# Sigmoid attention and an MLP on one core: the keys in chunks of 128 rows, the last 64 rows of two heads together

## The chip, the cores and the metric

The kernel runs on one NeuronCore of a Trainium2 chip. The metric is device time in microseconds (us). Three timed runs of the kernel before gave 1116.61 to 1118.22 us, median 1117.94.

## The reference

```python
B, H, S, D = 8, 12, 448, 64
scores = q @ k.T / sqrt(D) - log(S)            # per batch and head
attn   = sigmoid(scores)
y      = attn @ v
x = y.transpose(0, 2, 1, 3).reshape(B * S, H * D)     # 3584 tokens of 768
h = x @ w_in                                   # 768 -> 2048
g = h * sigmoid(1.702 * h)
out = g @ w_out                                # 2048 -> 768
```

q, k, v and x are float32. The two weight matrices come as float64; they go to the chip as pairs of 32-bit words and are made into float32 there. There is no softmax, so a row of scores needs no maximum and no sum.

## The kernel before

**Number formats.** Most products run in a rounded float32 format (`F32R`). A float32 operand is split into a rounded part and a rest, and a product is three matmuls: high by rest, rest by high, high by high. The product of attention and v is done in plain float32, for which TensorE gets two instructions per product.

**The attention.** The work is cut into 48 pairs of heads (8 batches by 6 pairs). Of a pair, q and k lie with the depth on the partitions, head 0 in partitions 0 to 63 and head 1 in 64 to 127, q in columns 0 to 447 and k in columns 448 to 895 of one tile. `split_pair` splits that tile (a cast, on ScalarE or VectorE, L340 or L341, and a subtraction on VectorE, L346). k's 448 rows are cut into NC = 4 chunks of C = 112 rows. For each chunk, `scores` (L518) issues three times two matmuls: those of the two heads use 64 rows of the array each, one the upper and one the lower half, and write two PSUM banks. One sigmoid on ScalarE (L529) reads both banks, 112 partitions by 896 columns. `values` (L541) then multiplies v's chunk by this: head 0 writes partitions 0 to 63, head 1 partitions 64 to 127 of one bank, with 112 rows of the array and 64 columns each. After the four chunks, that bank is copied into the tokens' tiles (L575 on ScalarE, L577 on VectorE), in one or two pieces, because a batch has 448 tokens and a block of the MLP has 512.

**PSUM banks.** Of the eight banks, six hold scores: tag `sc` has two buffers of two banks, tag `sc3` one, and the chunks take them in turn (`next(chunks) % 3`), whatever the pair. The other two, `av` and `m0`, take the sums of `values` of the odd and the even pairs.

**The order on TensorE.** A unit of the attention is the four chunks of scores of pair n, then the four chunks of values of pair n-1. The first units of the MLP (`h`, L686) may be placed between, but only at the end, since they need tokens and banks.

**The weights.** 32 tiles of weights, 768 KB each as float64, are loaded and decoded during the attention by some eight small operations each on VectorE and ScalarE (L393 to L427). The float32 result is stored to DRAM, and for half of them sums of weights are formed and stored as well.

**The planner.** `Plan` runs a list of tasks against costs given in the code and records, engine by engine, the order in which they are emitted; the order is then fixed. DMAs are all issued by SyncE, in one order. ScalarE, VectorE and SyncE take, of the tasks that are ready, the one whose result is needed soonest on TensorE. A load of weights has as its place in that list the split of a pair `PACE * i + 2` (`firsts`, the splits in order); it may be issued earlier if one of three buffers is free.

**The rest.** After the attention the MLP runs in blocks of tokens: block 0 by plain products (`h` and `o`), the others two at a time by a Strassen-like scheme (`two_blocks`). All its matmuls use 128 rows and 128 columns of the array and 512 moving columns.

Of the kernel before, what the change touches and what calls it, by code (L numbers as in the profile page):

```python
# [9 lines left out]
F32 = mybir.dt.float32  # L10
# [6 lines left out]
U64 = mybir.dt.uint64  # L17
AF = mybir.ActivationFunctionType
ALU = mybir.AluOpType

P = 128


T = 512

PACE = 1.3


SOON, PATIENCE = 6, 0.8
# [6 lines left out]
    sc=2, sc3=1, av=1, m=2, m0=1,  # L36
# [29 lines left out]
class Plan:  # L66
# [10 lines left out]
    def buffer(self, tag):  # L77
        b = Buffer()
        self.rings.setdefault(tag, []).append(b)
        return b  # L80

    def task(self, engine, cost, emit, deps=(), uses=()):
        return self.either({engine: cost}, {engine: emit}, deps, uses)
# [159 lines left out]
def sigmoid_attention_mlp(ctx: ExitStack, tc: tile.TileContext, qk, v, w, out):  # L243
# [2 lines left out]
    D = 64  # L246
    H = HD // D
    NP = H // 2
    S = S2 // 2
    NB = out.shape[0]  # L250
    NM = out.shape[1]
    NK = H * D // P
    NW = w.shape[0]
    NF = NW * NK // (NK + NM)

    NC = 4
    C = S // NC
    NW_EL = NK * P
    scale = 1.0 / math.sqrt(D)
    neg_log_s = -math.log(S)  # L260
# [45 lines left out]
    def make(b, tag, shape, dtype, name):  # L306
        if tag == "m" and tag not in spaces:
            early_bank.close()
            banks(tag, early_bank)
        if tag in LATE and tag not in spaces:  # L310
            att_stack.close()
            late = late_stack.enter_context(tc.tile_pool(name="late", bufs=2))
            for t in LATE:
                spaces[t] = late
        b.tile = spaces.get(tag, sb).tile(shape, dtype, tag=tag, name=name, bufs=BUFS[tag])
        return b.tile

    def dma(into, src, kb, deps, uses, first=lambda: None):
        def emit():
            first()  # L320
            nc.sync.dma_start(out=into(), in_=src())  # L321

        return task("SP", kb, emit, deps, uses)
# [48 lines left out]
    def decode(n):  # L372

        tag = "raw64"
        raw, e, sg = buffer(tag), buffer("e"), buffer("e")

        def take():
            make(raw, tag, [P, 2 * NW_EL], F32, f"w64_{n}")

        def words():  # L380
            r = raw.tile.bitcast(U64)
            pair = r.bitcast(U32).rearrange("p (n t) -> p n t", t=2)
            top = r.bitcast(U16).rearrange("p (n t) -> p n t", t=4)[:, :, 3]
            return pair[:, :, 0], pair[:, :, 1], top

        load = dma(lambda: raw.tile.bitcast(U64), lambda: w[n], 2 * KB, [], [raw], take)
        load.landing += 1.5
        plan.early.append((load, firsts[min(2 + int(PACE * len(decoded)), len(firsts) - 1)]))


        def exponent():
            make(e, "e", [P, NW_EL], U16, f"expo{n}")
            nc.vector.tensor_scalar(e.tile, words()[2], 0x7FF0, None, op0=ALU.bitwise_and)  # L393

        def sign():
            make(sg, "e", [P, NW_EL], BF16, f"sign{n}")
            nc.scalar.activation(sg.tile, words()[2].bitcast(I16), AF.Sign)  # L397

        t_e = task("DVE", 0.56, exponent, [load], [e, raw])
        t_s = task("ACT", 0.92, sign, [load], [sg, raw])  # L400
        t_b = task("DVE", 0.35, lambda: nc.vector.tensor_scalar(
            e.tile, e.tile, 896.0 * 16, 1151.0 * 16, op0=ALU.max, op1=ALU.min), [t_e], [e])
        t_x = on_either(
            (0.84, lambda: nc.scalar.activation(e.tile, e.tile, AF.Copy, scale=8.0, bias=-896.0 * 128)),
            (0.35, lambda: nc.vector.tensor_scalar(
                e.tile, e.tile, 896.0 * 16, 8.0, op0=ALU.subtract, op1=ALU.mult)),
            [t_b], [e],
        )
        t_g = task("DVE", 0.56, lambda: nc.vector.tensor_tensor(
            e.tile.bitcast(BF16), e.tile.bitcast(BF16), sg.tile, op=ALU.mult), [t_x, t_s], [e, sg])  # L410


        f = buffer("g")

        def f32():
            return f.tile[:, :NW_EL]

        def mantissa():
            make(f, "g", [P, 2 * T], F32, f"w32_{n}")
            nc.vector.tensor_scalar(  # L420
                f32().bitcast(U32), words()[1], 0xFFFFF, 0x100000, op0=ALU.bitwise_and, op1=ALU.bitwise_or
            )

        t_m = task("DVE", 0.56, mantissa, [load], [f, raw])
        t_l = task("DVE", 0.96, lambda: nc.vector.scalar_tensor_tensor(
            f32(), words()[0], 2.0**-32, f32().bitcast(I32), op0=ALU.mult, op1=ALU.add), [t_m], [f, raw])
        t_p = task("DVE", 0.96, lambda: nc.vector.scalar_tensor_tensor(  # L427
            f32(), f32(), 2.0**-20, e.tile.bitcast(BF16), op0=ALU.mult, op1=ALU.mult), [t_l, t_g], [f, e])
        decoded[n] = (t_p, f, f32)
        stored[n] = dma(lambda: whole[n], f32, KB, [t_p], [f])  # L430

    def two_parts(b, name, n, f, f32, deps):

# [40 lines left out]
    def load_pair(b, p):  # L474

        tag = "x"
        qkr, vr = buffer(tag), buffer("vraw")
        vals, rows = v[b], C
        t_q = dma(lambda: qkr.tile, lambda: qk[b, p * P : (p + 1) * P], P * S2 * 4 / 1024, [], [qkr],
                  lambda: make(qkr, tag, [P, S2], F32, f"qkraw{b}_{p}"))  # L480
        t_v = dma(lambda: vr.tile[:rows], lambda: vals[:, 2 * p : 2 * p + 2], rows * 8 * D * 4 / 1024, [], [vr],
                  lambda: make(vr, "vraw", [P, 2, NC, D], F32, f"vraw{b}_{p}"))
        return t_q, qkr, t_v, vr

    def split_pair(b, p, t_q, qkr):
# [7 lines left out]
        )  # L493
        return t, s


    chunks = itertools.count()
    last_early = []

    def scores(b, p, c, t_s, s, a):  # L500

        tag = "sc"
        if next(chunks) % 3 == 2:
            tag = "sc3"
        ps = buffer(tag)
        if tag == "sc3":
            last_early[:] = [ps]


        plain = (b, p) == (0, 0)  # L510
        terms = ((0, 0),) if plain else ((0, 1), (1, 0), (0, 0))

        def emit():
            make(ps, tag, [P, 2, 512], F32, f"sc{b}_{p}_{c}")
            src = [s.tile] if plain else [s.tile[:, 0], s.tile[:, 1]]
            for n, (kk, qq) in enumerate(terms):
                for j, rows in enumerate(halves_of_rows):
                    nc.tensor.matmul(  # L518
                        ps.tile[:C, j, :S],
                        lhsT=src[kk][rows, S + c * C : S + (c + 1) * C], rhs=src[qq][rows, :S],  # L520
                        start=n == 0, stop=n == len(terms) - 1,
                    )

        t = task("PE", 0.9 if plain else (0.7, 0.61, 0.61, 0.7)[c], emit, [t_s], [ps, s])

        def sigmoid():
            if a.tile is None:
                make(a, "a", [P, 2, 2, S], F32, f"a{b}_{p}_{c}")
            nc.scalar.activation(  # L529
                a.tile[:C, c % 2], ps.tile[:C, :, :S], AF.Sigmoid, bias=bias[:C], scale=scale  # L530
            )

        return t, task("ACT", 1.02, sigmoid, [t], [a, ps])

    def values(b, p, c, t_a, a, t_v, vr, ps, bank):

        def emit():
            if c == 0:
                make(ps, bank, [P, 512], F32, f"av{b}_{p}")
            for j, cols in enumerate(halves_of_rows):  # L540
                nc.tensor.matmul(  # L541
                    ps.tile[cols, :S], lhsT=vr.tile[:C, j, c], rhs=a.tile[:C, c % 2, j],
                    start=c == 0, stop=c == NC - 1,
                )

        return task("PE", (0.8, 0.75, 0.75, 0.85)[c], emit, [t_a, t_v], [ps, a, vr])

# [54 lines left out]
    def attention():  # L602

        units, late = [], []
        for n, (b, p) in enumerate(pairs):
            t_q, qkr, t_v, vr = load_pair(b, p)
            t_s, s = split_pair(b, p, t_q, qkr)
            bank = "av" if n % 2 else "m0"
            ps = buffer(bank)
            scored, next_late = [], []  # L610
            firsts.append(t_s)
            for half in range(2):
                a = buffer("a")
                got = [scores(b, p, c, t_s, s, a) for c in range(2 * half, 2 * half + 2)]
                scored.append([g[0] for g in got])
                next_late.append([
                    values(b, p, 2 * half + i, g[1], a, t_v, vr, ps, bank) for i, g in enumerate(got)
                ])

            for t in scored[1]:  # L620
                t.alone = False
            units.append(scored[0] + scored[1] + [t for two in late for t in two])
            to_x(b, p, next_late[1][1], ps)
            late = next_late
        units.append(late[0] + late[1])
        return units
# [545 lines left out]
```

## Time and profile before

| what | value |
|---|---|
| the profiled execution's own time | 1117.21 us |
| its span, first to last instruction | 1115.4 us |
| median of three timed runs | 1117.94 us |
| granted TensorE clock | 1.00 |
| TensorE matmuls busy | 1107.6 us (99%) |
| VectorE busy | 759.4 us (68%) |
| ScalarE busy | 508.1 us (46%) |
| first scores to the first `h` of the MLP | 4.25 to 295.47 us |

How to read it: the busy time of TensorE's matmuls (PE in the profile) says little here, since a matmul's end is modelled and one overlaps the next; how far apart two matmuls start says more. PEld is the loading of weights into the array. A group's row has the number of instructions, the busy time of the group and the mean of one, and behind the second bar the idle time of that engine just before them with what ended it. In a row of the timeline the first number is the start, the second how long the row lasts, both in us; equal instructions that follow each other make one row.

### The profile page before, as it was taken

To read this page: it belongs to the slowest core of one execution; us is meant where nothing else is said; L and a number is where in the kernel's file an instruction comes from. 1 tells how busy PE (TensorE), PEld (TensorE's weight loads), DVE (VectorE), ACT (ScalarE), POOL (GpSimd) and SP (SyncE) were. 2 spreads that over 40 slices of the span, in tenths; PEclk is the share of its full clock that TensorE was granted. 3 is DMA by queue.
4 is the path that set the end of the run, shared out by engine and by line. 5 is a ranking of instruction groups with operands and counts; after the bars stand their busy time and mean duration, and the time that the engine had idled before them with its cause. 6 is when DMAs were issued, how large, how long until landed. Compare 5 with 4: busy or idle time off the path is not lost.

```text
span 1115.4 us, 14973 instructions
## 1 busy us (share of the span) xinstructions
PE 1107.6 (99%) x5517; PEld 819.6 (73%) x5517; DVE 759.4 (68%) x1234; ACT 508.1 (46%) x729; POOL 0.2 (0%) x4
## 2 busy tenths in 40 slices
PE   8999999999999999999999999999999999999998
PEld 3544544545688888888888888888888888888887
DVE  6999999895496426887984664448864744477652
ACT  6988988888563322223633222225432322244220
POOL 0000000000000000000000000000000000000000
PEclk9999999999999999999999999999999999999999
DMA  9999999995455968666777975567669755556665
GB/s 330 333 375 375 388 400 395 385 338 162 151 188 182 358 216 321 246 244 216 254 227 223 307 242 191 195 198 250 216 208 310 255 188 191 195 174 214 207 202 194
DMA packets 113097, 285.69 MB, mean 256 GB/s; under 512 B 10368, under 2 KB 51328, under 8 KB 113024
## 3 DMA queue, kind: packets, MB, share of 16 engines
q1 hardware_dynamic: 113024, 284.73, 74.6%
q8 instruction: 44, 0.72, 0.3%
q14 instruction: 29, 0.24, 0.1%
HBM read 206.05 MB, written 78.64 MB: 255 GB/s over the span
## 4 chain that ended last, share of the span: by engine, by line
PE 96%; ACT 1%; DMA 1%; issue 0%; DVE 0%; SPq 0%; ACTq 0%; DVEq 0%
PE os L1059 18%; PE m L918 18%; PE oa L1059 13%; PE av L541 13%; PE sc L518 11%; PE sc L918 9%; PE h L686 6%; PE o L686 6%; PE av L918 4%; DMA qkraw<-qk 1%; ACT a L529 1%; SPq L321 0%; ACT sign L397 0%; DVE qk L346 0%; ACT qk L340 0%
## 5 line engine op out<-in xcount | busy, mean ns | idle before, releaser
L529 ACT ACTIVATE a<-sc,bias 112x896 f32<-112x896 f32 x192 | 183.0, 1006 | 42.8 <-PE av L541 30.4
L1059 PE MATMUL os<-gs,wds 128*128 128x512 f32 x864 | 196.3, 389 | 0.0
L1059 PEld LDWEIGHTS os<-gs,wds 128*128 128x128 f32 x864 | 162.2, 188 | 33.7
L541 PE MATMUL av<-a,vraw 112*64 112x448 f32 x768 | 154.7, 545 | 0.0
L1059 PE MATMUL oa<-ga,wda 128*128 128x512 f32 x648 | 147.4, 389 | 0.0
L1059 PEld LDWEIGHTS oa<-ga,wda 128*128 128x128 f32 x648 | 121.6, 188 | 25.3
L518 PE MATMUL sc<-qk 64*112 64x448 f32 x1128 | 137.4, 378 | 2.2 <-ACT a L529 2.1
L518 PEld LDWEIGHTS sc<-qk 64*112 64x112 f32 x1128 | 90.9, 171 | 63.3 <-ACT a L529 52.0
L541 PEld LDWEIGHTS av<-a,vraw 112*64 112x64 f32 x768 | 50.9, 136 | 82.3 <-issue 73.4
L918 PE MATMUL m<-x_s,w 128*128 128x512 f32 x468 | 109.3, 389 | 0.0
L918 PE MATMUL sc<-x,w 128*128 128x512 f32 x432 | 105.7, 389 | 0.0
L918 PEld LDWEIGHTS m<-x_s,w 128*128 128x128 f32 x468 | 87.8, 188 | 18.2
L918 PEld LDWEIGHTS sc<-x,w 128*128 128x128 f32 x432 | 81.1, 188 | 16.8
L880 ACT ACTIVATE g<-h 128x512 f32<-128x512 f32 x72 | 44.7, 632 | 91.1 <-DVE h L781 90.3
L340 ACT CAST gs<-gs 128x512 fp32r<-128x512 f32 x75 | 46.6, 623 | 84.5 <-PE os L1059 74.5
L686 PE MATMUL h<-x,wsplit 128*128 128x512 f32 x288 | 65.6, 389 | 0.0
L686 PE MATMUL o<-gs,wsplit 128*128 128x512 f32 x288 | 65.4, 389 | 0.0
L686 PEld LDWEIGHTS h<-x,wsplit 128*128 128x128 f32 x288 | 54.0, 188 | 11.9 <-issue 0.7
L686 PEld LDWEIGHTS o<-gs,wsplit 128*128 128x128 f32 x288 | 54.1, 188 | 11.2
L346 DVE TENSOR_TENSOR gs<-gs,gs 128x512 fp32r<-128x512 f32 x96 | 60.9, 686 | 0.4
L885 DVE TENSOR_TENSOR gs<-sc,g 128x512 f32<-128x512 f32 x24 | 16.6, 692 | 60.6 <-ACT g L880 60.6
L346 DVE TENSOR_TENSOR qk<-qkraw,qk 128x896 fp32r<-128x896 f32 x47 | 51.2, 1089 | 6.2 <-ACT qk L340 5.5
(94 smaller groups left out, 1204.1 us busy)
## 6 DMA issues: line engine op xcount, KB each, us to landing
w<-w SPq DMA_DIRECT2D x56, 768.0 KB, 6.6
wds<-t SPq DMA_DIRECT2D x72, 384.0 KB, 4.1
t<-t SPq DMA_DIRECT2D x32, 768.0 KB, 5.4
w<-t SPq DMA_DIRECT2D x32, 768.0 KB, 5.0
qkraw<-qk SPq DMA_DIRECT2D x48, 448.0 KB, 9.3
wda<-w SPq DMA_DIRECT2D x48, 384.0 KB, 4.0
f<-w SPq DMA_DIRECT2D x32, 384.0 KB, 8.1
w<-wsplit SPq DMA_DIRECT2D x16, 768.0 KB, 6.1
```

Source lines behind the costliest of these rows:

```text
L340: (costs[0], lambda: nc.scalar.copy(hi(), src())),
L346: lambda: nc.vector.tensor_tensor(lo(), src(), hi().bitcast(F32), op=ALU.subtract),
L518: nc.tensor.matmul(ps.tile[:C, j, :S], lhsT=src[kk][rows, S + c * C : S + (c + 1) * C], rhs=src[qq][rows, :S], start=n == 0, stop=n == len ...
L529: nc.scalar.activation(a.tile[:C, c % 2], ps.tile[:C, :, :S], AF.Sigmoid, bias=bias[:C], scale=scale)
L541: nc.tensor.matmul(ps.tile[cols, :S], lhsT=vr.tile[:C, j, c], rhs=a.tile[:C, c % 2, j], start=c == 0, stop=c == NC - 1,)
L686: nc.tensor.matmul(ps, lhsT=ws[a], rhs=x[:, c], start=first and i == 0, stop=last and i == 2)
L880: nc.scalar.activation(g.tile, h(), AF.Sigmoid, scale=1.702)
L885: nc.vector.tensor_tensor(gb.tile[:, block - one], h(), g.tile, op=ALU.mult)
L918: nc.tensor.matmul(ps, lhsT=ws[c], rhs=x[:, d], start=not more and i == 0 and j == 0, stop=i == NK // 2 - 1 and j == 2, skip_group_check=more,
L1059: nc.tensor.matmul(to, lhsT=w[c], rhs=x.tile[:, d], start=not more and i == 0 and j == 0, stop=i == len(rows) - 1 and j == 2, skip_group_c ...
```

## The change

Three things change.

**Chunks.** k's rows are taken in chunks of 128: of a head's 448 rows, three full chunks and 64 left over. The 64 left over of the two heads make one fourth chunk of 128 columns, with zeros in the other head's partitions, so that one matmul over all 128 rows of the array gives the scores of both: head 0 in partitions 0 to 63, head 1 in 64 to 127 of one bank. That chunk's three matmuls stand for six, and its sigmoid has 128 partitions by 448 columns. In `values` the fourth chunk multiplies 64 rows by 64 columns for each head, the first in the upper left quarter of the array and the second in the lower right. The tile of q and k has 960 columns instead of 896 (480 KB instead of 448), v's has the same bytes. The host arranges k and v so.

**Banks.** The chunks of scores take `sc`, `sc`, `sc3` and `m0` in that fixed order; the fourth needs one bank. The sums of `values` all take the one bank `av`.

**Weights.** `PACE` is 1.45 instead of 1.3, and a load of weights now waits for the split of a pair (`LEAD`). The store of the float32 weights of the first half (n < NF) waits for the split of the sixth last pair (`LATEST`).

```diff
-PACE = 1.3
+PACE, LEAD = 1.45, 1
+LATEST = 6
...
-    NC = 4
-    C = S // NC
+    NC = -(-S // P)
+    C = S - (NC - 1) * P
...
+        pair = int(PACE * len(decoded))
+        load = dma(lambda: raw.tile.bitcast(U64), lambda: w[n], 2 * KB, [firsts[pair - LEAD]] if pair >= LEAD else [],
+                   [raw], take)
...
-        stored[n] = dma(lambda: whole[n], f32, KB, [t_p], [f])
+        stored[n] = dma(lambda: whole[n], f32, KB, [t_p, *(firsts[-LATEST:][:1] if n < NF else [])], [f])
...
-        tag = "sc"
-        if next(chunks) % 3 == 2:
-            tag = "sc3"
+        tag = ("sc", "sc", "sc3", "m0")[c]
...
+                ends = dict(start=n == 0, stop=n == len(terms) - 1)
+                k = src[kk][:, S + c * P : S + (c + 1) * P]
+                if c == NC - 1:
+                    nc.tensor.matmul(ps.tile[:, :S], lhsT=k, rhs=src[qq][:, :S], **ends)
+                    continue
                 for j, rows in enumerate(halves_of_rows):
+                    nc.tensor.matmul(ps.tile[:, j, :S], lhsT=k[rows], rhs=src[qq][rows, :S], **ends)
...
+            if c == NC - 1:
+                to, scored = a.tile[:, c % 2, 0], ps.tile[:, :S]
+            else:
+                to, scored = a.tile[:, c % 2], ps.tile[:, :, :S]
+            nc.scalar.activation(to, scored, AF.Sigmoid, bias=bias, scale=scale)
...
+                if c == NC - 1:
+                    these, attn = vr.tile[cols, -D:], a.tile[cols, c % 2, 0]
+                else:
+                    at = (j * (NC - 1) + c) * D
+                    these, attn = vr.tile[:, at : at + D], a.tile[:, c % 2, j]
+                nc.tensor.matmul(ps.tile[cols, :S], lhsT=these, rhs=attn, start=c == 0, stop=c == NC - 1)
...
-            bank = "av" if n % 2 else "m0"
-            ps = buffer(bank)
+            ps = buffer("av")
```

TensorE, one unit in the last batch (`sc7_3_0` is chunk 0 of the scores of pair 3 of batch 7, `av7_2` the sum of values of pair 2; a row of `av` holds two chunks). Before:

```order
L518 MATMUL sc7_3_0_3198<-qk7_3_3130 112x448 x6
L518 MATMUL sc7_3_1_3208<-qk7_3_3130 112x448 x6
L518 MATMUL sc7_3_2_3218<-qk7_3_3130 112x448 x6
L518 MATMUL sc7_3_3_3226<-qk7_3_3130 112x448 x6
L541 MATMUL av7_2_3235<-a7_2_0_3162,vraw7_2_3096 64x448 x4
L541 MATMUL av7_2_3235<-a7_2_2_3191,vraw7_2_3096 64x448 x4
```

The same unit now:

```order
L527 MATMUL sc7_3_0_3057<-qk7_3_2984 128x448 x6
L527 MATMUL sc7_3_1_3067<-qk7_3_2984 128x448 x6
L527 MATMUL sc7_3_2_3078<-qk7_3_2984 128x448 x6
L524 MATMUL sc7_3_3_3086<-qk7_3_2984 128x448 x3
L553 MATMUL av7_2_3092<-a7_2_0_3016,vraw7_2_2955 64x448 x4
L553 MATMUL av7_2_3092<-a7_2_2_3043,vraw7_2_2955 64x448 x4
```

The order is the same; the fourth chunk has three matmuls instead of six.

ScalarE, from the copy of `av2_2` (the sums of pair 2 of batch 2) on; `a` is the output of a sigmoid, `x32` a tile of tokens, `qk` a split, `expo` a step of decoding. Before:

```order
L575 COPY x32_1_2_884<-av2_2_1256 128x128
L529 ACTIVATE a2_4_0_1294<-sc2_4_0_1283,bias_80 112x896
L529 ACTIVATE a2_4_0_1294<-sc2_4_1_1296,bias_80 112x896
L575 COPY x32_2_2_1327<-av2_2_1256 128x320
L340 CAST qk3_0_1329<-qkraw3_0_931 128x896
```

Now:

```order
L584 COPY x32_2_2_1229<-av2_2_1207 128x320
L409 ACTIVATE expo29_1178<-expo29_1178 128x768
L538 ACTIVATE a2_4_0_1254<-sc2_4_0_1231,bias_80 128x896
L538 ACTIVATE a2_4_0_1254<-sc2_4_1_1242,bias_80 128x896
L342 CAST qk3_0_1276<-qkraw3_0_936 128x960
```

The second piece of the copy stood behind the first two sigmoids of pair 4 (`a2_4`); now it stands ahead of them, and the other piece has gone to VectorE.

TensorE at the end of the attention, now (`h0_0` is the first product of the MLP; before, `av7_5` stood right behind `av7_4` and all of `h0_0` behind both):

```order
L553 MATMUL av7_4_3192<-a7_4_0_3133,vraw7_4_3064 64x448 x4
L553 MATMUL av7_4_3192<-a7_4_2_3157,vraw7_4_3064 64x448 x4
L694 MATMUL h0_0_3204<-x0_0_2804,wsplit0_1854 128x512 x3
L694 MATMUL h0_0_3204<-x0_1_2901,wsplit0_1854 128x512 x3
L553 MATMUL av7_5_3213<-a7_5_0_3178,vraw7_5_3122 64x448 x4
L553 MATMUL av7_5_3213<-a7_5_2_3199,vraw7_5_3122 64x448 x4
```

Six matmuls of `h0_0` have moved in front of the last pair's values.

More of the change, by code (lines that the diff above doesn't have):

```diff
@@ L248, in sigmoid_attention_mlp @@
     NP = H // 2
-    S = S2 // 2
+    S = out.shape[0] * T // B
     NB = out.shape[0]
@@ L384, in words @@
             return pair[:, :, 0], pair[:, :, 1], top
-        load = dma(lambda: raw.tile.bitcast(U64), lambda: w[n], 2 * KB, [], [raw], take)
+        pair = int(PACE * len(decoded))
+        load = dma(lambda: raw.tile.bitcast(U64), lambda: w[n], 2 * KB, [firsts[pair - LEAD]] if pair >= LEAD else [],
+                   [raw], take)
         load.landing += 1.5
-        plan.early.append((load, firsts[min(2 + int(PACE * len(decoded)), len(firsts) - 1)]))
+        plan.early.append((load, firsts[min(2 + pair, len(firsts) - 1)]))
         def exponent():
@@ L477, in load_pair @@
         qkr, vr = buffer(tag), buffer("vraw")
-        vals, rows = v[b], C
         t_q = dma(lambda: qkr.tile, lambda: qk[b, p * P : (p + 1) * P], P * S2 * 4 / 1024, [], [qkr],
                   lambda: make(qkr, tag, [P, S2], F32, f"qkraw{b}_{p}"))
-        t_v = dma(lambda: vr.tile[:rows], lambda: vals[:, 2 * p : 2 * p + 2], rows * 8 * D * 4 / 1024, [], [vr],
-                  lambda: make(vr, "vraw", [P, 2, NC, D], F32, f"vraw{b}_{p}"))
+        t_v = dma(lambda: vr.tile, lambda: v[b, p], P * S * 4 / 1024, [], [vr],
+                  lambda: make(vr, "vraw", [P, S], F32, f"vraw{b}_{p}"))
         return t_q, qkr, t_v, vr
@@ L494, in split_pair @@
         return t, s
-    chunks = itertools.count()
     last_early = []
     def scores(b, p, c, t_s, s, a):
-        tag = "sc"
-        if next(chunks) % 3 == 2:
-            tag = "sc3"
+        tag = ("sc", "sc", "sc3", "m0")[c]
         ps = buffer(tag)
@@ L513, in emit @@
         def emit():
-            make(ps, tag, [P, 2, 512], F32, f"sc{b}_{p}_{c}")
+            make(ps, tag, [P, 512] if c == NC - 1 else [P, 2, 512], F32, f"sc{b}_{p}_{c}")
             src = [s.tile] if plain else [s.tile[:, 0], s.tile[:, 1]]
             for n, (kk, qq) in enumerate(terms):
-                for j, rows in enumerate(halves_of_rows):
[L518 to L524, printed above, removed]
+                ends = dict(start=n == 0, stop=n == len(terms) - 1)
[3 more added lines that the diff above has]
+                    continue
+                for j, rows in enumerate(halves_of_rows):
+                    nc.tensor.matmul(ps.tile[:, j, :S], lhsT=k[rows], rhs=src[qq][rows, :S], **ends)
+        t = task("PE", 0.9 if plain else (0.7, 0.61, 0.61, 0.61)[c], emit, [t_s], [ps, s])
         def sigmoid():
@@ L528, in sigmoid, with values @@
                 make(a, "a", [P, 2, 2, S], F32, f"a{b}_{p}_{c}")
[L529 to L535, printed above, removed]
+            if c == NC - 1:
[3 more added lines that the diff above has]
+            nc.scalar.activation(to, scored, AF.Sigmoid, bias=bias, scale=scale)
+        return t, task("ACT", 0.6 if c == NC - 1 else 1.02, sigmoid, [t], [a, ps])
+    def values(b, p, c, t_a, a, t_v, vr, ps):
         def emit():
             if c == 0:
-                make(ps, bank, [P, 512], F32, f"av{b}_{p}")
+                make(ps, "av", [P, 512], F32, f"av{b}_{p}")
             for j, cols in enumerate(halves_of_rows):
[L541 to L544, printed above, removed]
+                if c == NC - 1:
[4 more added lines that the diff above has]
+                nc.tensor.matmul(ps.tile[cols, :S], lhsT=these, rhs=attn, start=c == 0, stop=c == NC - 1)
         return task("PE", (0.8, 0.75, 0.75, 0.85)[c], emit, [t_a, t_v], [ps, a, vr])
@@ L616, in attention @@
                 next_late.append([
-                    values(b, p, 2 * half + i, g[1], a, t_v, vr, ps, bank) for i, g in enumerate(got)
+                    values(b, p, 2 * half + i, g[1], a, t_v, vr, ps) for i, g in enumerate(got)
                 ])
@@ L1149 @@
     DM, DF = moe_w_in.shape
-    qk = np.concatenate([q, k], axis=2).transpose(0, 1, 3, 2)
-    qk = np.ascontiguousarray(qk).reshape(B, H * D, 2 * S)
-    vl = v.reshape(B, H, 4, S // 4, D).transpose(0, 3, 1, 2, 4)
+    full = S // P * P
+    last = np.zeros((B, H, P, D), np.float32)
+    last[:, 0::2, : S - full] = k[:, 0::2, full:]
+    last[:, 1::2, full - S :] = k[:, 1::2, full:]
+    qk = np.concatenate([q, k[:, :, :full], last], axis=2).transpose(0, 1, 3, 2)
+    qk = np.ascontiguousarray(qk).reshape(B, H * D, -1)
+    vh = v.reshape(B, H // 2, 2, S, D)
+    chunks = vh[:, :, :, :full].reshape(B, H // 2, 2, full // P, P, D).transpose(0, 1, 4, 2, 3, 5)
+    left = vh[:, :, :, full:].reshape(B, H // 2, 2 * (S - full), D)
+    vl = np.concatenate([chunks.reshape(B, H // 2, P, 2 * full // P * D), left], axis=3)
     vl = np.ascontiguousarray(vl)
```

## The prediction

> **What bounds the kernel now.** I read the page, then the windows, then the timeline of TensorE's weight loads and matmuls over one pair of the attention, and last ScalarE's timeline there. First the windows: 43 pairs of the attention, the time ahead of them, the last pair, and all that comes after.
>
> ```profile
> core 0: us, PE busy (x) PEld busy (x) DVE busy (x) ACT busy (x) POOL busy (x), PEclk, DMA share, GB/s
> 28.30:286.48 258.18, 257.45 (x1722) 129.02 (x1720) 224.76 (x379) 222.51 (x275) 0.00 (x0) 1.00 0.94 343
> 286.48:295.47 8.99, 8.99 (x58) 4.14 (x56) 1.25 (x2) 4.40 (x5) 0.00 (x0) 1.00 0.22 72
> 4.25:28.30 24.05, 22.55 (x136) 10.26 (x136) 17.14 (x27) 18.36 (x22) 0.00 (x0) 1.00 1.01 357
> 295.47:1115.00 819.53, 816.30 (x3602) 675.60 (x3600) 515.66 (x825) 261.38 (x427) 0.00 (x0) 1.00 0.69 228
> ```
>
> The MLP's 3600 matmuls take 819.53 us, 0.228 each; the change leaves their order and shapes alone, and I cost it at nothing there. The attention takes 258.18 / 43 = 6.004 us a pair, with VectorE 87% and ScalarE 86% busy. That looks like three engines near their limit. Which one sets the pace shows in a pair near the end, where VectorE has almost nothing to do (the second row above: 1.25 us in 8.99) and the pace is still the same. The weight loads of that pair:
>
> ```profile
> 286.48 1.69 PEld L518 LDWEIGHTS sc<-qk 64*112 64x112 f32 x18 [0.70 <-ACT a L529]
> 288.51 0.48 PEld L518 LDWEIGHTS sc<-qk 64*112 64x112 f32 x6 [0.34 <-ACT a L529]
> 289.31 0.20 PEld L541 LDWEIGHTS av<-a,vraw 112*64 112x64 f32 x4 [0.32 <-issue]
> 289.74 0.14 PEld L541 LDWEIGHTS av<-a,vraw 112*64 112x64 f32 x2 [0.23 <-issue]
> 290.12 0.14 PEld L541 LDWEIGHTS av<-a,vraw 112*64 112x64 f32 x2 [0.23 <-issue]
> ...
> 290.87 0.14 PEld L541 LDWEIGHTS av<-a,vraw 112*64 112x64 f32 x2 [0.23 <-issue]
> ```
>
> Three chunks of scores go through in one run (x18). The fourth (x6) starts only when ScalarE has read the first chunk of the same pair, since three buffers go round among four chunks. Single matmuls, from narrow windows at the same place, two rows for the change from values to scores, one inside the scores, two around the switch to values:
>
> ```profile
> 286.01 0.55 PE L541 MATMUL av<-a,vraw 112*64 112x448 f32 x2
> 286.78 0.37 PE L518 MATMUL sc<-qk 64*112 64x448 f32 x2
> 288.20 0.37 PE L518 MATMUL sc<-qk 64*112 64x448 f32 x2
> 289.01 0.37 PE L518 MATMUL sc<-qk 64*112 64x448 f32 x2
> ```
>
> From 286.78 to 288.20 are seven steps of two matmuls, 0.203 each; a step of values is (290.87 - 289.74) / 3 = 0.377. Against these steps there are three losses:
>
> - The wait for ScalarE: 288.20 to 288.51 is 0.31 instead of 0.20, and 288.51 to 289.01 is 0.50 for two steps instead of 0.41. Together 0.20, half of it the wait and half a restart with a weight load that nothing hides.
> - Scores to values: 289.01 to 289.31 is 0.30 instead of 0.20, and 289.31 to 289.74 is 0.43 instead of 0.38. Together 0.15.
> - Values to scores: 286.01 to 286.48 is 0.47 instead of 0.38, and 286.48 to 286.78 is 0.30 instead of 0.20. Together 0.19.
>
> 12 x 0.203 + 8 x 0.377 + 0.20 + 0.15 + 0.19 = 5.99: that is the pace, and in 43 pairs only about 1 us is lost beside it. So TensorE bounds the attention, ScalarE holds it in one place of each pair, and how busy ScalarE and VectorE are costs nothing by itself.
>
> **The change part by part.** *The bank of the fourth chunk.* It is `m0` now, which ScalarE freed a pair ago. ScalarE's rows of that pair say what else could hold it:
>
> ```profile
> 285.16 1.91 ACT L529 ACTIVATE a<-sc,bias 112x896 f32<-112x896 f32 x2 [1.78 <-PE av L541]
> 287.45 1.91 ACT L529 ACTIVATE a<-sc,bias 112x896 f32<-112x896 f32 x2 [0.38 <-PE sc L518]
> ```
>
> The sigmoids of the pair before end at 285.16 + 1.91 = 287.07, the fourth chunk comes at 288.20: no wait is left. -0.20 x 47 pairs with split operands = -9.4 us.
>
> *128 instead of 112 columns.* A matmul streams 448 columns either way, and three full matmuls stand for three couples: the same number of steps. Only the weight load that shows at the restart grows, from 0.10 by 16 / 112: +0.01 x 47 = +0.7.
>
> *Two new changes of shape.* Inside the scores the rows of the array go from 64 to 128 (columns stay), inside the values from 128 to 64 (columns stay). No such step is in this trace. At most it costs what the known switches cost. The one that ends in 128 columns is from values to the MLP:
>
> ```profile
> 295.00 0.55 PE L541 MATMUL av<-a,vraw 112*64 112x448 f32 x2
> 295.47 16.65 PEld L686 LDWEIGHTS h<-x,wsplit 128*128 128x128 f32 x74 [0.70 <-issue]
> 295.81 0.39 PE L686 MATMUL h<-x,wsplit 128*128 128x512 f32 x1
> 296.04 0.39 PE L686 MATMUL h<-x,wsplit 128*128 128x512 f32 x1
> ```
>
> 0.47 instead of 0.38, then 0.34 instead of 0.23: 0.20. So +0 to +0.20 in the scores, +0 to +0.15 in the values (64 columns, as from scores to values), together 0 to +0.35 a pair, +16.4 us over 47. A gain is excluded, since couples already run at one per 448 columns. I take nothing: all known switches change the columns and the number format as well, and the one from values to `h`, where the rows hardly change (112 to 128), loses the same 0.09 ahead of its load as the ones where they do. So the rows explain nothing in this trace; that they are free it does not show, and that is the largest risk. The Trainium skill, "TensorEngine Tiling (Array Packing)", section "Tiling Modes", speaks against this change: going from one tiling mode to another drains TensorE. No run here shows such a step of the rows alone; by that rule the sum would be the first rival's.
>
> *One bank for all sums.* Values of the next pair must wait until the last sums are copied. The time for that is the scores of the pair between, 286.48 to 289.31 = 2.83, now 2.63. A copy takes about half a microsecond; before, one could be late without harm:
>
> ```profile
> 101.38 1.91 ACT L529 ACTIVATE a<-sc,bias 112x896 f32<-112x896 f32 x2 [0.23 <-PE sc L518]
> 103.17 0.42 ACT L575 COPY x<-av 128x320 f32<-128x320 f32 x1
> 103.22 3.23 PE L541 MATMUL av<-a,vraw 112*64 112x448 f32 x16
> ```
>
> Here the copy ended at 103.59, after the next values had begun. In the new order copies stand ahead of those sigmoids; I cost it at nothing, up to (103.59 - 103.22) = 0.37 a pair if it fails.
>
> *ScalarE and VectorE.* The fourth sigmoid falls from about 1.01 to about 0.6 us (512 columns took 0.598), 0.4 x 48 = 19 us of ScalarE. VectorE's subtraction for the split grows by 64 / 896 of 1.089.
>
> ```profile
> L713 ACT ACTIVATE g<-h 128x512 f32<-128x512 f32 x16 | 9.6, 598 | 17.7 <-PE h L686 17.7
> L346 DVE TENSOR_TENSOR qk<-qkraw,qk 128x896 fp32r<-128x896 f32 x47 | 51.2, 1089 | 6.2 <-ACT qk L340 5.5
> ```
>
> That is 0.08 x 47 = 3.7 us, hidden under VectorE's 33 idle us of the 258. If pairs take 5.99 - 0.20 + 0.01 = 5.80 us, 43 of them take 249 and VectorE needs 228: 92%. Without that cover the most would be +3.7. In the steady stretch none of ScalarE's 19 us is on the path.
>
> *The start.* Here ScalarE does bound:
>
> ```profile
> 8.64 0.48 PEld L518 LDWEIGHTS sc<-qk 64*112 64x112 f32 x6 [0.43 <-ACT a L529]
> 9.54 0.47 PEld L518 LDWEIGHTS sc<-qk 64*112 64x112 f32 x6 [0.42 <-ACT a L529]
> 22.12 0.47 PEld L518 LDWEIGHTS sc<-qk 64*112 64x112 f32 x6 [1.29 <-ACT a L529]
> ```
>
> Chunks of the second pair come 0.90 apart, a sigmoid's length, instead of 0.61; later one waits for a sigmoid that stood behind steps of decoding. The window of 24.05 us holds four scores and three values; at the steps above (the first pair in plain float32, eight steps of 0.38) they need 3.0 + 3 x 2.44 + 3 x 3.01 + 6 switches of 0.17 = 20.4, so 3.6 are lost, 0.6 of them counted already. Shorter sigmoids, a fourth buffer and later weights should take half of the other 3.0: -1.5 (bounds 0 and -3).
>
> *The weights' pace, the late stores.* The DMA engines are at 0.94 in the stretch, and yet no load holds TensorE there. Loads that are issued later, and sixteen stores in the last six pairs, are queued on SyncE ahead of loads of v; those have over two pairs' time. I cost them at nothing, +2 at most.
>
> *The end.* Six matmuls of `h` between the last two values add two switches, +0.20 + 0.15 = +0.35; they cover the wait for the one bank, some 1 us.
>
> Sum: -9.4 + 0.7 - 1.5 + 0.35 = -9.9. The profiled execution's own time is 1117.21 (span 1115.4), 0.7 under the median of the runs, 1117.94. So 1107.3 for a profile like this one and 1108.0 for the median.
>
> **The rivals.**
>
> 1. *Changes of rows cost a switch.* Each pair pays 0.35 where it saves 0.20; the pace is 5.99 - 0.20 + 0.01 + 0.35 = 6.15. That is +16.4 on 1108.0: 1124.4, slower. For it: every switch in the trace costs 0.15 to 0.20, as if the array had to empty and load in the open. Against it: none of them is of rows alone. It decides from 0.20 a pair, the two together.
> 2. *Only one of the two costs.* With the scores alone +0.20 x 47 = +9.4: 1117.4, no change. With the values alone +0.15 x 47 = +7.0: 1115.0, just faster.
> 3. *Quarters don't run together, or copies are late.* If the two 64x64 matmuls of the fourth values ran one after the other, two steps of 0.38 more a pair: +36 us, 1144. Late copies at 0.37 a pair: +17, 1125. Against the first: halves of rows and halves of columns both run in couples here.
> 4. *The change doesn't do what it says:* the fourth chunk's bank is free, and an order with VectorE at 92% makes TensorE wait as long elsewhere: 1116 to 1119.
>
> **How the numbers follow.** Forecast 0.48, rival 1 0.31, rival 2 0.11, rival 3 0.06, rival 4 0.04. A measurement of this kernel tells some 0.2%, 2.2 us, from no change. Faster: the forecast and half of rival 2, 0.53. Slower: rivals 1 and 3, 0.37. Within: half of rival 2 and rival 4, 0.10. The forecast's own range is 1104 to 1112: down by the start at -3, the stray 1 us and the 1.3 us that the fastest run lies under the median, up by the start at 0 and 3 for VectorE and the queues. The whole range goes from 1104 to 1125; it leaves out the upper part of rival 1 and most of rival 3.
>
> **What would show it.** In the profile after: the four chunks of a pair's scores in one run without a wait for ScalarE; the pace 5.80 us; the step into the fourth chunk 0.20 (rival 1: 0.30, and the next 0.30); the fourth values' first step 0.38 (rival 1: 0.47, then 0.43); the attention as a whole some 10 us shorter. I am wrong if the pace is 5.99 or more, or if VectorE's or ScalarE's copies end TensorE's waits.

## The result and the profile after

| | before | changed |
|---|---|---|
| median of four runs, us | 1117.28 (1115.94 to 1118.22) | 1124.29 (1122.47 to 1125.29) |
| ratio to before | | 1.0062, 95% interval 1.0044 to 1.0080 |
| span of the profiled execution, us | 1115.4 | 1120.7 |

The change makes the kernel slower by some 7 us. That is the first rival's time (1124.4), not the forecast's (1108.0). That it is met to 0.1 us is partly luck. The profiled execution is the fastest of the four, 1122.47 us: for one like the profile before, that rival's sum gives 0.7 less than 1124.4, 1123.7.

The windows of the profile after, cut at the same places as before (the start of the fifth pair's scores, the last pair's, and the values' end):

```profile
4.23:26.42 22.19, 22.19 (x125) 10.77 (x125) 17.33 (x27) 18.32 (x22) 0.00 (x0) 1.00 1.02 397
26.42:291.00 264.58, 264.58 (x1593) 131.69 (x1591) 221.47 (x367) 219.56 (x286) 0.00 (x0) 1.00 0.93 339
291.00:302.18 11.18, 11.14 (x62) 5.08 (x60) 0.00 (x0) 4.57 (x7) 0.00 (x0) 1.00 0.28 94
302.18:1120.00 817.82, 814.93 (x3596) 674.69 (x3594) 514.60 (x824) 262.85 (x428) 0.00 (x0) 1.00 0.69 228
```

The same 43 pairs take 264.58 us instead of 258.18: 6.153 a pair, +6.4 in all. TensorE's busy time fills that window to the last digit: the profile records no wait of it there. The start is 1.9 us shorter (26.42 instead of 28.30). The stretch from the last pair's scores to the first `o` of the MLP, here before and after, is 0.8 longer:

```profile
286.48:360.89 74.41, 74.41 (x346) 58.31 (x345) 54.45 (x82) 35.91 (x58) 0.00 (x0) 1.00 0.53 181
...
291.00:366.23 75.23, 75.19 (x343) 58.13 (x342) 52.68 (x79) 37.09 (x61) 0.00 (x0) 1.00 0.52 178
```

-1.9 + 6.4 + 0.8 = 5.3 is the whole difference of the two spans. The medians differ by 7.0; the other 1.7 us stand in neither profile.

The weight loads of one pair after the change (scores are L527 and, for the fourth chunk, L524; values L553):

```profile
149.49 1.72 PEld L527 LDWEIGHTS sc<-qk 64*128 64x128 f32 x18 [0.71 <-ACT a L538]
151.51 0.51 PEld L524 LDWEIGHTS sc<-qk 128*128 128x128 f32 x3 [0.30 <-ACT sign L402]
152.33 0.20 PEld L553 LDWEIGHTS av<-a,vraw 128*64 128x64 f32 x4 [0.31 <-ACT a L538]
...
153.89 0.14 PEld L553 LDWEIGHTS av<-a,vraw 128*64 128x64 f32 x2 [0.23 <-issue]
154.74 0.19 PEld L553 LDWEIGHTS av<-a,vraw 64*64 64x64 f32 x4 [0.70 <-issue]
155.63 0.18 PEld L527 LDWEIGHTS sc<-qk 64*128 64x128 f32 x2 [0.70 <-ACT a L538]
```

Loads that follow one another without a gap are those that hide under the matmul ahead; a gap of 0.3 behind scores, or 0.70 behind values, is a load that had to wait. Before there were three such gaps in a pair. Now there are four: ahead of the fourth scores (151.51), ahead of the values, ahead of the fourth values (154.74), and ahead of the next scores. What the view prints behind the first, a step of decoding, feeds nothing there; it only ended last. The matmuls around the two new gaps, from narrow windows:

```profile
151.22 0.37 PE L527 MATMUL sc<-qk 64*128 64x448 f32 x2
151.51 0.48 PE L524 MATMUL sc<-qk 128*128 128x448 f32 x1
151.83 0.37 PE L524 MATMUL sc<-qk 128*128 128x448 f32 x1
154.26 0.55 PE L553 MATMUL av<-a,vraw 128*64 128x448 f32 x2
155.16 0.54 PE L553 MATMUL av<-a,vraw 64*64 64x448 f32 x2
```

A step is the time from the start of one matmul, or of one couple (the two heads' matmuls side by side), to the start of the next. Into the fourth scores it is 0.29 and then 0.32, where a step takes 0.20; into the fourth values 154.74 - 154.26 = 0.48 and then 0.42, where a step takes 0.38. That is 0.21 and 0.14 a pair, 0.35 together, against the 0.20 that the removed wait gave back.

### The profile page after: what moved, and what is told of

It reads as the page before. It is cut to its first block, busy times and chain, and to the rows that moved or that the text cites. A ratio compares the mean times of both kernels' runs of the same rounds, so it can differ in the third digit from the quotient of the medians.

```text
span 1120.7 us, 14633 instructions
## 1 busy us (share of the span) xinstructions
PE 1115.2 (100%) x5374; PEld 822.8 (73%) x5374; DVE 753.9 (67%) x1220; ACT 506.8 (45%) x743; POOL 0.2 (0%) x4
## 4 chain that ended last, share of the span: by engine, by line
PE 99%; DMA 0%; DVE 0%; issue 0%
PE os L1067 17%; PE m L926 17%; PE av L553 14%; PE oa L1067 13%; PE sc L527 9%; PE sc L926 9%; PE h L694 6%; PE o L694 6%; PE av L926 4%; PE sc L524 3%; DMA qkraw<-qk 0%; DVE p L789 0%
## 5 line engine op out<-in xcount | busy, mean ns | idle before, releaser
L538 ACT ACTIVATE a<-sc,bias 128x896 f32<-128x896 f32 x192 | 164.8, 912 | 41.6 <-PE av L553 33.8
L553 PE MATMUL av<-a,vraw 128*64 128x448 f32 (+1 forms) x768 | 162.0, 551 | 0.0
L553 PEld LDWEIGHTS av<-a,vraw 128*64 128x64 f32 (+1 forms) x768 | 46.4, 135 | 93.2 <-issue 86.8
L527 PEld LDWEIGHTS sc<-qk 64*128 64x128 f32 x846 | 75.7, 184 | 38.6 <-ACT a L538 33.1
L527 PE MATMUL sc<-qk 64*128 64x448 f32 x846 | 99.0, 375 | 0.0
L348 DVE TENSOR_TENSOR qk<-qkraw,qk 128x960 fp32r<-128x960 f32 x47 | 54.2, 1154 | 2.4 <-ACT qk L342 2.0
```

The costliest lines, as they stand in the source:

```text
L348: lambda: nc.vector.tensor_tensor(lo(), src(), hi().bitcast(F32), op=ALU.subtract),
L527: nc.tensor.matmul(ps.tile[:, j, :S], lhsT=k[rows], rhs=src[qq][rows, :S], **ends)
L538: nc.scalar.activation(to, scored, AF.Sigmoid, bias=bias, scale=scale)
L553: nc.tensor.matmul(ps.tile[cols, :S], lhsT=these, rhs=attn, start=c == 0, stop=c == NC - 1)
```

## The experiments

Theory 1: whenever the part of the array that a matmul uses changes, in rows or in columns, TensorE pays some 0.09 us and a weight load that nothing hides. The rivals are named with each run. The times of before beside them, on the same chips, are 1117.19 us for the first four runs and 1117.46 for the others.

**e1_values128: the fourth values with 128 rows.**

```diff
-                    these, attn = vr.tile[cols, -D:], a.tile[cols, c % 2, 0]
+                    at = (2 * (NC - 1) + j) * D
+                    these, attn = vr.tile[:, at : at + D], a.tile[:, c % 2, 0]
...
+    left = np.zeros((B, H // 2, P, 2, D), np.float32)
+    left[:, :, : S - full, 0] = vh[:, :, 0, full:]
+    left[:, :, full - S :, 1] = vh[:, :, 1, full:]
```

> The fourth chunk's values use 128 rows of the array again, the other head's rows being zeros, so that the rows no longer change inside the values; the scores keep their full matmul. Theory 1, a change of the array's rows costs as much as any other change of the matmul's shape (0.20 us into 128 columns, 0.15 into 64): the pace falls from 6.15 to 6.00 us a pair, 0.15 x 47 = 7.0 us less than the changed kernel's 1124.3, so about 1117.3, and the first step into the fourth values is 0.38 instead of 0.47. Rival, the loss belongs to the fourth chunk itself (its bank, its waits, zeros in the operands): the pace stays at 6.15 and the time at 1124.

For the zeros, v's tile has 512 columns instead of 448, and the planner finds another order for VectorE and ScalarE; so it is in e3, e4 and e8 too.

Measured 1118.77 us, ratio to before 1.0012 (1.0003 to 1.0021). The loads of its fourth values (128.28 is one of them) and its 43 pairs:

```profile
127.53 0.14 PEld L554 LDWEIGHTS av<-a,vraw 128*64 128x64 f32 x2 [0.23 <-issue]
127.90 0.14 PEld L554 LDWEIGHTS av<-a,vraw 128*64 128x64 f32 x2 [0.23 <-issue]
128.28 0.14 PEld L554 LDWEIGHTS av<-a,vraw 128*64 128x64 f32 x2 [0.23 <-issue]
129.13 1.71 PEld L527 LDWEIGHTS sc<-qk 64*128 64x128 f32 x18 [0.70 <-ACT a L538]
...
27.24:287.20 259.96, 257.87 (x1593) 137.65 (x1592) 218.93 (x361) 221.63 (x292) 0.00 (x0) 1.00 0.95 350
```

The gap is gone, the steps are 0.38 throughout. TensorE's own work is 257.87 / 43 = 6.00 us a pair, as theory 1 has it. Another 2.1 us (259.96 - 257.87) are two waits, of the kind that e3 shows, and enough for the 1.5 us by which the time lies above 1117.3.

**e2_scores64: the fourth scores with 64 rows.**

```diff
-                    nc.tensor.matmul(ps.tile[:, :S], lhsT=k, rhs=src[qq][:, :S], **ends)
+                    rows = halves_of_rows[0]
+                    nc.tensor.matmul(ps.tile[:, :S], lhsT=k[rows], rhs=src[qq][rows, :S], **ends)
```

> The fourth chunk's scores use 64 rows of the array like the other three, by leaving out the last 64 keys of head 1 (so its part of the result is left out); bank, columns, moving size and waits are as in the changed kernel, and the values keep their quarters. Theory 1: the step into the fourth scores is 0.20 instead of 0.30 and the next 0.20 instead of 0.31; the pace falls from 6.15 to 5.95 us, 0.20 x 47 = 9.4 less than 1124.3, so about 1114.9. Rival, the new bank or its wait restarts TensorE: the steps and the time stay, 6.15 and 1124.

Measured 1114.15 us, ratio 0.9977 (0.9967 to 0.9987).

```profile
127.94 1.72 PEld L528 LDWEIGHTS sc<-qk 64*128 64x128 f32 x18 [0.70 <-ACT a L539]
129.67 0.59 PEld L525 LDWEIGHTS sc<-qk 64*128 64x128 f32 x3
...
27.07:282.21 255.14, 255.14 (x1593) 135.39 (x1592) 220.91 (x367) 217.99 (x286) 0.00 (x0) 1.00 0.94 351
```

The fourth chunk's loads (x3) follow the others without a gap, though bank, waits and columns are the changed kernel's: 255.14 / 43 = 5.93 us. The rival, a restart by the new bank, falls. This run also shows that no wait for ScalarE is left in the scores.

**e3_both: both edits.**

> Both of these edits together (the last 64 keys of head 1 are left out of the scores): no change of rows inside scores or inside values. Theory 1: pace 5.80 us, 0.35 x 47 = 16.4 less than 1124.3, so about 1107.9, which is what the prediction said of the change itself. Rival, other waits (copies out of the one bank, VectorE at 92%) come up once TensorE is faster: more than 5.85 us a pair, 1110 to 1117.

Measured 1110.17 us, ratio 0.9940 (0.9925 to 0.9955). The window of 43 pairs, then TensorE's waits in the middle of the attention:

```profile
26.99:278.71 251.72, 249.02 (x1593) 138.98 (x1592) 219.11 (x363) 220.66 (x292) 0.00 (x0) 1.00 0.96 362
...
PE av L555 <- issue: 1.4, 1, 1.4
PE av L555 <- ACT x L586: 1.3, 1, 1.3
...
152.09 0.42 DVE L588 COPY x<-av 128x256 f32<-128x256 f32 x1
...
152.62 0.60 PE L555 MATMUL av<-a,vraw 128*64 128x448 f32 x2 [1.41 <-issue]
```

249.02 / 43 = 5.79: the pace of the forecast, to 0.01. The rival comes in as well, in a small way: twice the values wait for a copy out of their one bank (the last two rows are the first time: the copy ends at 152.51, the values start at 152.62), 2.7 us in all, about what is missing to 1107.9.

**e4_cols: a change of columns alone.**

```diff
+            if c == NC - 1:
+                nc.tensor.matmul(ps.tile[:, :S], lhsT=vr.tile[:, -2 * D :], rhs=a.tile[:, c % 2, 0], start=False, stop=True)
+                return
```

> The fourth chunk's values as one matmul of 128 rows by 128 columns for both heads (v's rows of one head are zeros in the other's columns) instead of two in quarters: inside the values the rows stay at 128, the columns change from 64 to 128, the number format stays float32. Theory 1, any change of shape costs: 0.20 us where the changed kernel pays 0.15, so a pace of 6.20 us and about 1126.7. Rival, only a change of rows (or of the number format) costs: 6.00 us and 1117.3.

Measured 1128.44 us, ratio 1.0098 (1.0083 to 1.0113).

```profile
130.26 0.14 PEld L553 LDWEIGHTS av<-a,vraw 128*64 128x64 f32 x2 [0.23 <-issue]
131.11 0.30 PEld L548 LDWEIGHTS av<-a,vraw 128*128 128x128 f32 x2 [0.70 <-issue]
...
26.66:295.10 268.44, 266.59 (x1506) 136.55 (x1505) 219.07 (x361) 224.16 (x292) 0.00 (x0) 1.00 0.92 340
```

The gap of 0.70 is back, with 128 columns to load instead of 64: 266.59 / 43 = 6.20 us a pair, 0.20 over e1's 6.00. So it isn't rows as such: columns alone cost too. Two waits for copies, 1.9 us (268.44 - 266.59), are about what the time lies above 1126.7.

**e5_format: a change of the number format alone.**

```diff
-        terms = ((0, 0),) if plain else ((0, 1), (1, 0), (0, 0))
+        terms = ((0, 0),) if plain or c == 1 else ((0, 1), (1, 0), (0, 0))
...
+            return t.bitcast(F32) if c == 1 and not plain else t
```

> The kernel before, with the second chunk of scores as one plain float32 product of the rounded parts (two of the three terms are left out): inside the scores the number format changes twice, rows and columns never. If a change of format costs, the steps into the second and into the third chunk are 0.30 us and the ones behind them longer too; if only the matmul's shape counts, they are what the matmul ahead takes: 0.20 into the second chunk, 0.38 into the third. The two float32 steps of 0.38 stand for three of 0.20, +0.14 a pair; that is longer than the 0.11 for which the fourth chunk waits, so its 0.20 should go: a pace of 5.93 us if the format is free (about 1114), 6.2 if each change costs 0.15 (about 1127).

One execution, 1116.37 us. From narrow windows: the last matmuls of the first chunk, the first float32 ones, and the first and second of the third chunk.

```profile
154.29 0.36 PE L521 MATMUL sc<-qk 64*112 64x448 f32 x2
154.49 0.54 PE L521 MATMUL sc<-qk 64*112 64x448 f32 x2
154.89 0.71 PE L521 MATMUL sc<-qk 64*112 64x448 f32 x2
155.44 0.36 PE L521 MATMUL sc<-qk 64*112 64x448 f32 x2
```

Into float32 it is 0.20. From the first float32 couple to the third chunk's second is 155.44 - 154.49 = 0.95, what two float32 steps and one rounded one take (0.38 + 0.38 + 0.20 = 0.96). The format is free, both ways, to the 0.01 us that the rows show. That takes away the escape that the prediction left open (all known switches change the format as well). The pace and the time did not come out, though. The 43 pairs and the loads of one fourth chunk:

```profile
28.19:285.71 257.52, 257.18 (x1636) 121.48 (x1634) 224.82 (x379) 222.55 (x275) 0.00 (x0) 1.00 0.94 345
...
131.94 0.47 PEld L521 LDWEIGHTS sc<-qk 64*112 64x112 f32 x6 [0.19 <-ACT a L532]
```

257.52 / 43 = 5.99 us a pair, not 5.93, and 1116.37 us, not 1114. It is far from the 6.2 of a format that costs. The fourth chunk's loads still stand behind a gap, so its loss did not go whole.

**e6_weights and e7_chunks: the two halves of the change.** The first is the kernel before with the new `PACE`, `LEAD` and `LATEST`, the second the changed kernel without them.

> The kernel before with the new pace of the weights alone (PACE, LEAD, LATEST). The pace of a pair stays at 5.98; if later weights are what saved the start, its 2 us come here: about 1115. If the shorter sigmoids or the fourth buffer saved them: 1117, as before.

> The changed kernel with the old pace of the weights. Pace 6.15 us as changed; if later weights saved the start, some 2 us more than the changed kernel's 1124.3, about 1126; if the chunks did, 1124.

The weights alone: 1116.05 us, ratio 0.9986 (0.9976 to 0.9995). The chunks alone: 1130.43 us, ratio 1.0114 (1.0099 to 1.0129). So -1.4 and +13.0; they don't add up to the +7.0 of the two together, and the second expectation missed by more than 4 us. The first came out between its two values, 1115 and 1117. With the weights alone the fifth pair starts at 27.42, 0.9 us earlier than before, and the pace stays (257.78 / 43 = 5.995):

```profile
27.42:285.20 257.78, 257.56 (x1723) 128.99 (x1721) 221.72 (x374) 224.76 (x279) 0.00 (x0) 1.00 0.96 344
```

TensorE's longest waits in e7, and VectorE and TensorE at the first of them:

```profile
PE av L553 <- ACT a L538: 2.0, 1, 2.0
PE av L553 <- issue: 1.1, 1, 1.1
PE av L553 <- DVE x L586: 1.0, 1, 1.0
...
191.61 0.56 DVE L414 TENSOR_TENSOR expo<-expo,sign 128x768 bf16<-128x768 bf16 x1 [2.02 <-ACT sign L402]
...
194.76 0.35 DVE L586 COPY x<-av 128x192 f32<-128x192 f32 x1
...
195.21 1.31 PE L553 MATMUL av<-a,vraw 128*64 128x448 f32 x5 [2.00 <-ACT a L538]
```

VectorE stands 2 us waiting for a step of decoding on ScalarE, and behind that step in its order stands the copy out of the one bank; the values start when it is done (194.76 + 0.35, then 195.21), not at the sigmoid that the row names. Over the attention that adds up to 270.08 - 264.85 = 5.2 us:

```profile
28.85:298.93 270.08, 264.85 (x1593) 132.13 (x1591) 220.57 (x367) 224.65 (x287) 0.00 (x0) 1.00 0.89 329
```

With the weights asked for later there is no such wait in the changed kernel (264.58 of 264.58 busy). The one bank does make the copies urgent, then. Whether they come in time hangs on the order that the planner finds. Later weights alone do not see to it: e1, e3 and e4 have them too and wait 2.1, 2.7 and 1.9 us. What in e7 brought the waits, the earlier loads, the earlier stores or the new order as such, is not shown.

**e8_shape: the leftover keys in the shape of the values.** The fourth scores become one float32 product of 128 rows by 64 columns a head, from the tile before the split; the values are those of e1.

```diff
-                    nc.tensor.matmul(ps.tile[:, :S], lhsT=k, rhs=src[qq][:, :S], **ends)
+                    for cols in halves_of_rows:
+                        nc.tensor.matmul(ps.tile[cols, :S], lhsT=k[:, cols], rhs=src[qq][:, :S], **ends)
```

> The whole computation, with the last 64 keys in the shape of the values: the fourth chunk's scores as one plain float32 product from the unsplit tile, 128 rows by 64 columns, head 0 into partitions 0 to 63 and head 1 into 64 to 127 as a couple, and its values with 128 rows and zeros. Theory 1: the only changes of shape are the two that the kernel before has too, the step from the fourth scores into the values is a plain 0.38; steps 0.31 + 7 x 0.20 + 0.30 + 0.43 + 8 x 0.38 + 0.47 make a pace of 5.93 us, 0.22 x 47 = 10.3 less than 1124.3: 1114, faster than both kernels. Rival: the change of format or the first step into a product of values costs in any case, 6.08 us a pair, 1121.

Measured 1115.17 us, ratio 0.9981 (0.9972 to 0.9991): faster than both kernels, by 2.3 and some 9 us.

```profile
128.03 1.72 PEld L528 LDWEIGHTS sc<-qk 64*128 64x128 f32 x18 [0.70 <-ACT a L539]
130.05 0.20 PEld L525 LDWEIGHTS sc<-qkraw 128*64 128x64 f32 x4 [0.30 <-ACT a L539]
130.48 0.14 PEld L555 LDWEIGHTS av<-a,vraw 128*64 128x64 f32 x2 [0.23 <-issue]
130.86 0.14 PEld L555 LDWEIGHTS av<-a,vraw 128*64 128x64 f32 x2 [0.23 <-issue]
...
26.98:283.22 256.24, 255.81 (x1636) 127.83 (x1634) 219.17 (x364) 219.47 (x287) 0.00 (x0) 1.00 0.94 355
```

One gap stands between the third chunk (x18) and the fourth; from there into the values (130.48, 130.86) the steps are plain 0.38. 256.24 / 43 = 5.96 us; the steps that the expectation lists add up to 5.95, not to the 5.93 that it names.

## Why the prediction was wrong

**The step that failed** is "I take nothing" under "Two new changes of shape": a cost put at 0 of a range of 0 to 0.35 us a pair. Measured is the upper end, 0.21 + 0.14 = 0.35, 16 us over 47 pairs. The reason given for the lower end was that the switch from values to `h`, where the rows hardly change, loses as much as those where they do, "so the rows explain nothing". That does not follow: if any change costs a fixed 0.09 and a load, a second change in the same step adds nothing either, and all three known switches look just the same. The runs show it to be so. Into 64 columns, rows alone cost 0.14, and rows, columns and format together cost 0.15 (scores to values). Into 128 columns, rows alone cost 0.21, columns alone 0.20 (e4). Taken away, the loss goes (e1, e2), and the format has no part in it (e5). What the array does in the 0.09 us no run shows. The rule that the prediction quoted from the Trainium skill, "TensorEngine Tiling (Array Packing)", section "Tiling Modes", is that a change of mode drains TensorE, that is, lets it run empty first. The trace agrees in that no change of shape is free: 0.14 us into 64 columns, 0.21 into 128.

The other steps:

- *TensorE bounds the attention, ScalarE's load does not.* Right. The sigmoids of 192 chunks take 164.8 instead of 183.0 us, and the attention is longer even so: its pace is that of TensorE's steps. The row after counts the 48 short ones under the shape of the others:

```profile
L538 ACT ACTIVATE a<-sc,bias 128x896 f32<-128x896 f32 x192 | 164.8, 912 | 41.6 <-PE av L553 33.8
```

- *The wait in the fourth chunk, -0.20.* Right: without the change of rows, in e2, there is no gap.
- *Pace.* The rival's was 6.15, measured 6.153; the forecast's 5.80 is e3's 5.79, once no shape changes.
- *One bank, nothing, up to 0.37 a pair.* Right for the kernel as changed, but it hangs on the order: in other orders the copies cost 5.2 us (e7), 2.7 (e3), 2.1 (e1) and 1.9 (e4).
- *The weights' pace, nothing.* Wrong in size: 1130.43 - 1124.29 = 6.1 us in its favour with the new chunks, most of it the copies' waits, and 1.4 with the old ones.
- *The start, -1.5.* The fifth pair starts 1.9 us earlier, about 2.3 with the slower pace of its three intervals taken off. From the second pair's scores to the fifth's it is 20.56 us before (7.74 to 28.30), 19.82 with the weights alone (7.60 to 27.42), 18.40 with the chunks alone (10.45 to 28.85) and 18.45 with both (7.97 to 26.42). So the chunks alone can bring all of it. That is not quite clean: in e7 the first pair is slow, as the last section shows, which gives the other engines more time.
- *The end, +0.35.* 0.8. The last two values also have their fourth chunk in quarters, 2 x 0.15, which makes it 0.65; the rest is not accounted for.

## What to carry over

Where matmuls stand back to back, look at how far apart they start, not at busy time: a matmul that uses fewer instructions, or leaves less to the engine behind it, can still lose more than it saves if it uses the array in another shape than its neighbours. Try a leftover piece in the shape of what stands before or behind it, with zeros or in another number format if need be; here both were cheaper than a switch. And where two readings of the known switches fit a trace equally well, the one that costs nothing has no better claim.

## What was not expected of the hardware

The attention's first matmuls, plain float32, take 0.37 us a step in the profiles of the kernels before and after, of e4 and of e6, but 0.75 in those of e1, e2, e3, e5, e7 and e8. After, and e7, whose first pair is the same:

```profile
5.06 0.19 PEld L527 LDWEIGHTS sc<-qkraw 64*128 64x128 f32 x2 [0.32 <-issue]
5.43 0.19 PEld L527 LDWEIGHTS sc<-qkraw 64*128 64x128 f32 x2 [0.19 <-issue]
```

```profile
5.96 0.34 PEld L527 LDWEIGHTS sc<-qkraw 64*128 64x128 f32 x2 [0.41 <-issue]
6.71 0.34 PEld L527 LDWEIGHTS sc<-qkraw 64*128 64x128 f32 x2 [0.41 <-issue]
```

Half the rate for the first microseconds, and the pairs behind come later: the second pair's scores start at 7.97 after, at 9.26 in e1 and at 10.45 in e7. The granted clock in the profile's windows is 1.00 in all of them. The Trainium skill, "TensorE: Matmul & The Clock Gate", Part 1, says that the array starts at half its clock and that the moment of the change differs from run to run. The steps agree with that, the printed clock does not show it. So a difference of 1 or 2 us at the start of this kernel cannot be read from one profile each. The 1.7 us by which the medians differ more than the profiles may come from there too; those executions left no trace, so that is not shown.
